# A GeGLU feed-forward layer: eight half-size products of the down projection become seven

## The chip, the core and the metric

The kernel runs on one core of a Trainium2 chip. The core has a matrix engine (TensorE, PE in the profile; its weight loads are listed apart as PEld), a vector engine (VectorE, DVE), an activation engine (ScalarE, ACT), GpSimd (POOL) and a queue engine (SyncE, SP) that issues most DMA transfers. Working data lies in SBUF, matrix results in PSUM, which has eight banks of 128 x 512 fp32 values. The metric is device time in microseconds of one execution; the time before is the median of five runs.

## The reference

The layer has 1024 tokens (32 x 32), width D = 1024 and inner width F = 3584. All inputs and the output are bf16.

```python
def _gelu(x):
    return jax.nn.gelu(x, approximate=True)

def reference(x, w_gate, w_up, w_down):
    return (_gelu(x @ w_gate) * (x @ w_up)) @ w_down
```

These are three products of the same size: x times w_gate, x times w_up, and the gated result g (1024 x 3584) times w_down (3584 x 1024).

## The kernel before

A tile is 128 rows or columns: F has 28 of them (FT), the tokens 8, D has 8. One matmul instruction multiplies a stationary 128 x 128 block (loaded by a weight load) by a moving block of up to 512 columns and adds the result to one PSUM bank.

**First stage.** x is brought in transposed (xT). The first quarter of D for the first 512 tokens is transposed on TensorE, the rest comes by transposing DMAs on SP. The weights w_gate and w_up are loaded in seven chunks of four F-tiles (1 MB each for wg and wu) into two rotating buffers. For each F-tile and each block of 512 tokens, 8 matmuls make a gate bank and 8 an up bank (`mm1`, line 117). `eltwise` (lines 125 to 138) turns the two banks into 512 columns of gT: ACT copies the gate (L127) and squares it (L129), DVE makes the argument of a sigmoid in two operations (L131, L133), ACT evaluates the sigmoid (L135), DVE multiplies with the up bank (L137) and with the sigmoid (L138). The eight PSUM banks hold four such pairs, so TensorE can be up to three pairs ahead of the elementwise work. The first chunk is written out by hand in another order ("head", lines 186 to 195): its four F-tiles share the pieces of x and the weights as they arrive.

w_down (wd, 7 MB) is loaded whole on SP, in seven loads of 1 MB, `load_wd`, during the first stage.

**Second stage.** `mm2_block` (line 209) takes one token tile and one half of D, accumulates 28 matmuls (line 212) in a bank, with gT stationary and wd moving, then DVE casts the bank to bf16 (L220) and ACT issues the store (L221). 8 token tiles by 2 halves give 16 blocks; the last one is cut in a block of 384 and one of 128 columns, which makes 17.

**Order.** TensorE's order around the head is as written (`manual_schedule` for that engine); the other engines are ordered by the framework's planner. Each engine and each DMA queue takes its instructions in order: one that waits holds up what is behind it.

Of the kernel before, what the change touches and what calls it, by code (L numbers as in the profile page):

```python
# [8 lines left out]
ACT = mybir.ActivationFunctionType  # L9
ALU = mybir.AluOpType  # L10

_C2 = 2.0 * 0.7978845608028654
_A = 0.044715
_C2A = _C2 * _A
# [3 lines left out]
def kernel(  # L18
# [8 lines left out]
    nc = tc.nc  # L27
    P = nc.NUM_PARTITIONS
    fp32 = mybir.dt.float32
    bf16 = mybir.dt.bfloat16  # L30

    xf = x.flatten_outer_dims()
    of = out.flatten_outer_dims()
    N, D = xf.shape
    F = w_gate.shape[1]
    assert D % P == 0 and F % P == 0 and N % P == 0
    DT = D // P
    FT = F // P
    NT = N // P
    MM_N = 512  # L40
    NB = min(N, MM_N)
    assert N % NB == 0
    NNB = N // NB
    DB = min(D, MM_N)
    assert D % DB == 0
    NDB = D // DB

    FC = 4
    assert FT % FC == 0 and DT % 4 == 0
    NCH = FT // FC  # L50
    KQ = DT // 4
    NWARM = 6
# [2 lines left out]
    wu_r = w_up.rearrange("(dt dp) f -> dp dt f", dp=P)  # L55
    wd_r = w_down.rearrange("(ft fp) d -> fp ft d", fp=P)

    xpool = ctx.enter_context(tc.tile_pool(name="xT", bufs=1))
    gpool = ctx.enter_context(tc.tile_pool(name="gT", bufs=1))
    wdpool = ctx.enter_context(tc.tile_pool(name="wd", bufs=1))  # L60
    wpool = ctx.enter_context(tc.tile_pool(name="w", bufs=2))
    ework = ctx.enter_context(tc.tile_pool(name="ework", bufs=3))
    opool = ctx.enter_context(tc.tile_pool(name="osb", bufs=3))
    cpool = ctx.enter_context(tc.tile_pool(name="const", bufs=1))
    pspool = ctx.enter_context(tc.tile_pool(name="psum", bufs=8, space=bass.MemoryType.PSUM))

    xT = xpool.tile([P, DT, N], bf16, name="xT")
    gT = gpool.tile([P, FT, N], bf16, name="gT")
    wd = wdpool.tile([P, FT, D], bf16, name="wd")

    ones_w = nc.const_aps.tensor(1.0, [P, P], bf16)
    ones_m = nc.const_aps.tensor(1.0, [P, NB], bf16)
    warm_ps = pspool.tile([P, NB], fp32, name="warm_ps", tag="acc")
# [3 lines left out]
    HALF = NB_P // 2  # L77
# [9 lines left out]
    def alloc_w_chunk(ci):  # L87
        w_tiles[ci] = (
            wpool.tile([P, DT, FC * P], bf16, name="wg", tag="wg"),
            wpool.tile([P, DT, FC * P], bf16, name="wu", tag="wu"),  # L90
        )

    def load_w(eng, ci, which, d0, d1):
        src = (wg_r, wu_r)[which]
        f0 = ci * FC * P
        eng.dma_start(out=w_tiles[ci][which][:, d0:d1, :], in_=src[:, d0:d1, f0 : f0 + FC * P])

    def load_w_chunk(ci):
        alloc_w_chunk(ci)
        for which in (0, 1):  # L100
            load_w(nc.sync, ci, which, 0, DT)

    def load_xT(t0, t1, d0, d1):
        nc.sync.dma_start_transpose(out=xT[:, d0:d1, t0:t1], in_=xf[t0:t1, d0 * P : d1 * P])

    def load_wd(ci):
        fsl = slice(ci * FC, (ci + 1) * FC)
        nc.sync.dma_start(out=wd[:, fsl, :], in_=wd_r[:, fsl, :])

    def weights_of(ft):  # L110
        fl = ft % FC
        fsl = slice(fl * P, (fl + 1) * P)
        return [t[:, :, fsl] for t in w_tiles[ft // FC]]

    def mm1(ps, wt, t0, tw, d0=0, d1=DT):
        for dt in range(d0, d1):
            nc.tensor.matmul(  # L117
                ps,
                lhsT=wt[:, dt, :],
                rhs=xT[:, dt, t0 : t0 + tw],  # L120
                start=(dt == 0),
                stop=(dt == DT - 1),
            )

    def eltwise(ft, t0, tw, gate_ps, up_ps):
        h = ework.tile([P, NB], bf16, name="h", tag="h")[:, :tw]
        nc.scalar.activation(h, gate_ps, ACT.Copy)  # L127
        sq = ework.tile([P, NB], bf16, name="sq", tag="sq")[:, :tw]
        nc.scalar.activation(sq, gate_ps, ACT.Square)  # L129
        w = ework.tile([P, NB], bf16, name="w", tag="w")[:, :tw]  # L130
        nc.vector.tensor_scalar(w, sq, _C2A, _C2, ALU.mult, ALU.add)  # L131
        z = ework.tile([P, NB], bf16, name="z", tag="z")[:, :tw]
        nc.vector.tensor_tensor(z, w, h, ALU.mult)  # L133
        s = ework.tile([P, NB], bf16, name="s", tag="s")[:, :tw]
        nc.scalar.activation(s, z, ACT.Sigmoid)  # L135
        hu = ework.tile([P, NB], bf16, name="hu", tag="hu")[:, :tw]
        nc.vector.tensor_tensor(hu, h, up_ps, ALU.mult)  # L137
        nc.vector.tensor_tensor(gT[:, ft, t0 : t0 + tw], hu, s, ALU.mult)  # L138

    def pair(tw):  # L140
        return (
            pspool.tile([P, NB], fp32, name="gate_ps", tag="acc")[:, :tw],
            pspool.tile([P, NB], fp32, name="up_ps", tag="acc")[:, :tw],
        )

    def mm1_and_eltwise(ft, t0, tw):
        ps = pair(tw)
        for p, wt in zip(ps, weights_of(ft)):
            mm1(p, wt, t0, tw)
        eltwise(ft, t0, tw, *ps)  # L150

    alloc_w_chunk(0)
    for dt in range(KQ):
        load_w((nc.sync, nc.scalar)[dt % 2], 0, 0, dt, dt + 1)
    load_w(nc.scalar, 0, 1, 0, KQ)
    for q in range(1, 4):
        d0, d1 = q * KQ, (q + 1) * KQ
        load_xT(0, NB, d0, d1)
        load_w(nc.sync, 0, 0, d0, d1)
        load_w(nc.sync, 0, 1, d0, d1)  # L160
    for nb in range(1, NNB):
        for q in range(2):
            load_xT(nb * NB, (nb + 1) * NB, 2 * q * KQ, 2 * (q + 1) * KQ)
    load_w_chunk(1)
    load_wd(0)

    with tc.manual_schedule(engines={mybir.EngineType.PE}):
        for _ in range(NWARM):
            nc.tensor.matmul(warm_ps, lhsT=ones_w, rhs=ones_m, start=True, stop=True)  # L169
        for dt in range(KQ):  # L170
            for half in range(2):
                hw = HALF * P
                tp = pspool.tile([P, hw], bf16, name="tp", tag="acc")
                for b in range(HALF):
                    nc.tensor.transpose(  # L175
                        tp[:, b * P : (b + 1) * P],
                        x_nat[:, half * HALF + b, dt * P : (dt + 1) * P],
                        ident,
                    )
                dst = xT[:, dt, half * hw : (half + 1) * hw]  # L180
                if half == 0:
                    nc.vector.tensor_copy(dst, tp)  # L182
                else:
                    nc.scalar.copy(dst, tp)  # L184
        nc.tensor.matmul(warm_ps[:, : NB // 2], lhsT=ones_w, rhs=ones_m[:, : NB // 2], start=True, stop=True)  # L185
        head = [pair(NB) for _ in range(FC)]
        for q in range(3):
            for which in (0, 1):
                for dt in range(q * KQ, (q + 1) * KQ):
                    for ft in range(FC):  # L190
                        mm1(head[ft][which], weights_of(ft)[which], 0, NB, dt, dt + 1)
        for ft in range(FC):
            for which in (0, 1):
                mm1(head[ft][which], weights_of(ft)[which], 0, NB, 3 * KQ, DT)
            eltwise(ft, 0, NB, *head[ft])

    for ft in range(FC):
        for nb in range(1, NNB):
            mm1_and_eltwise(ft, nb * NB, NB)

    for ci in range(1, NCH):
        if ci + 1 < NCH:
            load_w_chunk(ci + 1)
        load_wd(ci)
        for fl in range(FC):
            for nb in range(NNB):
                mm1_and_eltwise(ci * FC + fl, nb * NB, NB)

    def mm2_block(tsl, dsl):
        out_ps = pspool.tile([P, dsl.stop - dsl.start], fp32, name="out_ps", tag="acc")  # L210
        for ft in range(FT):
            nc.tensor.matmul(  # L212
                out_ps,
                lhsT=gT[:, ft, tsl],
                rhs=wd[:, ft, dsl],
                start=(ft == 0),
                stop=(ft == FT - 1),
            )
        o_sb = opool.tile([P, DB], bf16, name="o_sb", tag="o_sb")[:, : dsl.stop - dsl.start]
        nc.vector.tensor_copy(o_sb, out_ps)  # L220
        nc.scalar.dma_start(out=of[tsl, dsl], in_=o_sb)  # L221

    for tt in range(NT):
        tsl = slice(tt * P, (tt + 1) * P)
        for db in range(NDB):
            if tt == NT - 1 and db == NDB - 1 and DB > P:
                cut = (db + 1) * DB - P
                mm2_block(tsl, slice(db * DB, cut))
                mm2_block(tsl, slice(cut, (db + 1) * DB))
            else:  # L230
                mm2_block(tsl, slice(db * DB, (db + 1) * DB))


# [28 lines left out]
```

## Time and profile before

| | |
|---|---|
| median of five runs | 300.26 us (299.43 to 300.54) |
| the profiled execution | 300.19 us |
| its span, first to last instruction | 298.4 us |
| TensorE busy | 294.6 us (99%) |
| VectorE, ScalarE busy | 108.8 us (36%), 98.2 us (33%) |
| matmuls of the two up projections | 896, from 4.7 to 198.5 us |
| matmuls of the down projection | 476, from 198.5 to 295.2 us |
| DMA moved | 26.43 MB, mean 89 GB/s |

A group's line shows the program line, the engine and operation, output and inputs, the shape and the count, then the busy time in us and the mean duration in ns of one instruction, then the idle time of the engine just before them and what ended it. A matmul's duration includes its way through the array, which overlaps with that of the next; how often one starts is read from the chain in order of time. Line numbers are those of the kernel before.

### The profile page before, as it was taken

What the parts mean: (1) busy time and instruction counts of PE and PEld (TensorE: products, weight loads), DVE (VectorE), ACT (ScalarE), POOL (GpSimd) and SP (SyncE); (2) the same over time, 40 slices, a digit from 0 to 9 for tenths busy, and PEclk for the clock granted to TensorE, in tenths of its full rate; (3) what the DMA queues carried; (4) which work ended last, traced back from release to release, by engine and by line L of the source; (5) the groups of instructions that cost most, each with busy time, mean ns of one, the idle gap of its engine ahead of it and who ended that gap; (6) DMA issues with size and microseconds to landing.
All of it is one profiled execution on the core that took longest, in us unless ns stands there. A gap on an engine that the chain in (4) does not pass through costs nothing.

```text
span 298.4 us, 3493 instructions
## 1 busy us (share of the span) xinstructions
PE 294.6 (99%) x1387; PEld 134.7 (45%) x1387; DVE 108.8 (36%) x243; ACT 98.2 (33%) x172; POOL 0.7 (0%) x6
## 2 busy tenths in 40 slices
PE   8999999999999999999999999999999999999996
PEld 3444444444444444444444444444444444444444
DVE  0057654445554445554445555440010001100111
ACT  2087544554544554544554454540000000000000
POOL 0000000000000000000000000000000000000000
PEclk9999999999999999999999999999999999999999
DMA  7999996080026005300800000000001000000001
GB/s 162 313 282 379 387 366 227 0 281 2 0 74 207 2 0 170 111 2 2 279 4 0 0 0 2 0 0 18 20 18 35 18 20 18 34 21 18 18 18 37
DMA packets 28703, 26.43 MB, mean 89 GB/s; under 512 B 8208, under 2 KB 25104, under 8 KB 28688
## 3 DMA queue, kind: packets, MB, share of 16 engines
q1 hardware_dynamic: 25552, 23.60, 24.7%
q10 hardware_dynamic: 3136, 2.62, 2.9%
q8 instruction: 11, 0.18, 0.2%
q14 instruction: 4, 0.03, 0.0%
HBM read 22.28 MB, written 2.10 MB: 82 GB/s over the span
## 4 chain that ended last, share of the span: by engine, by line
PE 98%; DMA 1%; DVE 0%; issue 0%
PE gate_ps L117 32%; PE up_ps L117 32%; PE out_ps L212 32%; DMA x_nat<-in_x_dram 1%; PE tp L175 0%; DVE o_sb L220 0%; PE warm_ps L185 0%
## 5 line engine op out<-in xcount | busy, mean ns | idle before, releaser
L117 PE MATMUL gate_ps<-xT,wg 128*128 128x512 bf16 x448 | 106.6, 380 | 0.0
L117 PE MATMUL up_ps<-xT,wu 128*128 128x512 bf16 x448 | 106.3, 379 | 0.0
L212 PE MATMUL out_ps<-wd,gT 128*128 128x512 bf16 (+2 forms) x476 | 96.9, 366 | 0.0
L212 PEld LDWEIGHTS <-gT 128*128 128x128 bf16 x476 | 45.5, 98 | 51.6
L117 PEld LDWEIGHTS <-wg 128*128 128x128 bf16 x448 | 43.9, 98 | 52.9 <-issue 0.3
L117 PEld LDWEIGHTS <-wu 128*128 128x128 bf16 x448 | 43.8, 98 | 53.1 <-DMA wu<-in_w_up_dram 0.5
L127 ACT ACTIVATE h<-gate_ps 128x512 bf16<-128x512 f32 x56 | 33.4, 597 | 52.3 <-PE gate_ps L117 52.3
L135 ACT ACTIVATE s<-z 128x512 bf16<-128x512 bf16 x56 | 35.3, 630 | 46.1 <-DVE z L133 46.1
L131 DVE TENSOR_SCALAR w<-sq 128x512 bf16<-128x512 bf16 x56 | 16.5, 294 | 74.6 <-ACT sq L129 74.5
L137 DVE TENSOR_TENSOR hu<-h,up_ps 128x512 bf16<-128x512 bf16 x56 | 38.2, 681 | 12.0 <-ACT h L127 12.0
L220 DVE CAST o_sb<-out_ps 128x512 bf16<-128x512 f32 (+2 forms) x17 | 11.2, 660 | 84.4 <-PE out_ps L212 84.4
L129 ACT ACTIVATE sq<-gate_ps 128x512 bf16<-128x512 f32 x56 | 33.1, 592 | 0.0
L138 DVE TENSOR_TENSOR gT<-hu,s 128x512 bf16<-128x512 bf16 x56 | 23.8, 426 | 9.9 <-ACT s L135 9.9
L133 DVE TENSOR_TENSOR z<-w,h 128x512 bf16<-128x512 bf16 x56 | 23.8, 425 | 1.8
L169 PE MATMUL warm_ps<-const-bfloat16-1.0 128*128 128x512 bf16 x6 | 2.7, 624 | 0.8 <-PEq L246 0.8
L182 DVE COPY xT<-tp 128x256 bf16<-128x256 bf16 x2 | 0.6, 293 | 4.2 <-PE tp L175 4.2
L184 ACT ACT_TABLE_LOAD x1 | 1.3, 1283 | 2.3 <-issue 2.3
L169 PEld LDWEIGHTS <-const-bfloat16-1.0 128*128 128x128 bf16 x6 | 0.7, 132 | 1.9 <-issue 1.9
L135 ACT ACT_TABLE_LOAD x1 | 1.3, 1283 | 0.0
L175 PEld LDWEIGHTS <-x_nat 128*128 128x128 bf16 x8 | 0.7, 130 | 1.1 <-DMA x_nat<-in_x_dram 1.0
L175 PE MATMUL tp<-ident,x_nat 128*128 128x128 bf16 x8 | 1.1, 307 | 0.1
L184 ACT COPY xT<-tp 128x256 bf16<-128x256 bf16 x2 | 0.7, 372 | 0.8 <-PE tp L175 0.7
(8 smaller groups left out, 1.5 us busy)
## 6 DMA issues: line engine op xcount, KB each, us to landing
wd<-in_w_down_dram SPq DMA_DIRECT2D x7, 1024.0 KB, 14.0
wg<-in_w_gate_dram SPq DMA_DIRECT2D x6, 1024.0 KB, 5.3
wu<-in_w_up_dram SPq DMA_DIRECT2D x6, 1024.0 KB, 7.3
out_dram<-o_sb ACTq DMA_DIRECT2D x15, 128.0 KB, 1.7
wg<-in_w_gate_dram SPq DMA_DIRECT2D x3, 256.0 KB, 3.8
wu<-in_w_up_dram SPq DMA_DIRECT2D x3, 256.0 KB, 4.2
wu<-in_w_up_dram ACTq DMA_DIRECT2D x1, 256.0 KB, 5.0
x_nat<-in_x_dram ACTq DMA_DIRECT2D x1, 128.0 KB, 3.1
```

The lines of the kernel that those rows point to most:

```text
L117: nc.tensor.matmul(ps, lhsT=wt[:, dt, :], rhs=xT[:, dt, t0 : t0 + tw], start=(dt == 0), stop=(dt == DT - 1),)
L127: nc.scalar.activation(h, gate_ps, ACT.Copy)
L129: nc.scalar.activation(sq, gate_ps, ACT.Square)
L131: nc.vector.tensor_scalar(w, sq, _C2A, _C2, ALU.mult, ALU.add)
L133: nc.vector.tensor_tensor(z, w, h, ALU.mult)
L135: nc.scalar.activation(s, z, ACT.Sigmoid)
L137: nc.vector.tensor_tensor(hu, h, up_ps, ALU.mult)
L138: nc.vector.tensor_tensor(gT[:, ft, t0 : t0 + tw], hu, s, ALU.mult)
L169: nc.tensor.matmul(warm_ps, lhsT=ones_w, rhs=ones_m, start=True, stop=True)
L184: nc.scalar.copy(dst, tp)
L212: nc.tensor.matmul(out_ps, lhsT=gT[:, ft, tsl], rhs=wd[:, ft, dsl], start=(ft == 0), stop=(ft == FT - 1),)
L220: nc.vector.tensor_copy(o_sb, out_ps)
```

## The change

Three things change.

**The down projection.** g and w_down are cut in halves: A11 and A12 are the tokens 0 to 511 with the F-tiles 14 to 27 and 0 to 13, A21 and A22 the tokens 512 to 1023 likewise; B11, B12 are the rows of the F-tiles 14 to 27 of w_down with the columns 0 to 511 and 512 to 1023, B21, B22 those of the F-tiles 0 to 13. Eight products of such halves would give the output. The new kernel makes seven (Winograd's form of Strassen's method): A12 B21, A11 B11, S1 T1, S2 T2, S3 T3, A22 T4 and S4 B22, in this order. The sums are

- S1 = A21 + A22, S2 = S1 - A11, S3 = A11 - A21, S4 = A12 - S2
- T1 = B12 - B11, T2 = B22 - T1, T3 = B22 - B12, T4 = B21 - T2

A half-size product is 4 token tiles (m) by 14 F-tiles (k) of 128 x 128 x 512 matmuls. It occupies four PSUM banks; there are two sets of four, banka and bankb, and several products accumulate on top of an earlier one in the same set. Copies of a bank's intermediate state are taken by ACT into SBUF (`snap`), and DVE adds them to the final banks when it writes the output (`store`).

The sums are made on DVE from bf16 into tiles of type float32r (4 bytes). The five products with a sum in them run with both operands in float32r; for two of these ACT copies A22 and B22 into float32r tiles. S2 and T2, T4 and S4 are made in place. S1 and T1 are made during the first stage, the other sums during the second.

**The loads of w_down.** It is no longer kept whole in SBUF. A ring of four buffers of 512 KB (`wdring`) receives batches of four F-tiles by 512 columns (the last of a half has two F-tiles). Each batch is loaded on SP when it is wanted, several of them more than once: 8 loads in the first stage, 28 in the second. A load waits until the reader of the buffer four loads earlier is done.

**GELU and order.** `eltwise` is one GELU activation on ACT and one product on DVE. All engines, not TensorE alone, keep the order in which the program is written.

The core of the diff, with the first stage's unchanged lines left out:

```diff
     def eltwise(ft, t0, tw, gate_ps, up_ps):
         h = ework.tile([P, NB], bf16, name="h", tag="h")[:, :tw]
-        nc.scalar.activation(h, gate_ps, ACT.Copy)
-        sq = ework.tile([P, NB], bf16, name="sq", tag="sq")[:, :tw]
-        nc.scalar.activation(sq, gate_ps, ACT.Square)
-        w = ework.tile([P, NB], bf16, name="w", tag="w")[:, :tw]
-        nc.vector.tensor_scalar(w, sq, _C2A, _C2, ALU.mult, ALU.add)
-        z = ework.tile([P, NB], bf16, name="z", tag="z")[:, :tw]
-        nc.vector.tensor_tensor(z, w, h, ALU.mult)
-        s = ework.tile([P, NB], bf16, name="s", tag="s")[:, :tw]
-        nc.scalar.activation(s, z, ACT.Sigmoid)
-        hu = ework.tile([P, NB], bf16, name="hu", tag="hu")[:, :tw]
-        nc.vector.tensor_tensor(hu, h, up_ps, ALU.mult)
-        nc.vector.tensor_tensor(gT[:, ft, t0 : t0 + tw], hu, s, ALU.mult)
+        nc.scalar.activation(h, gate_ps, ACT.Gelu_apprx_tanh)
+        nc.vector.tensor_tensor(g_of(ft)[:, t0 : t0 + tw], h, up_ps, ALU.mult)
...
+    HF = FT // 2
+    HT = N // 2
+    MT = HT // P
+    KB = 4
+    batches = [(k, min(k + KB, HF)) for k in range(0, HF, KB)]
+    hi, lo = HF, 0
+    A11, A12 = [[g[:, :, :HT] for g in gs] for gs in (g_hi, g_lo)]
+    A21, A22 = [[g[:, :, HT:] for g in gs] for gs in (g_hi, g_lo)]
+
+    def load_b(f_off, col, b):
+        k0, k1 = b
+        t = wdring.tile([P, KB, DB], bf16, name="wdb", tag="wdb")
+        nc.sync.dma_start(
+            out=t[:, : k1 - k0, :],
+            in_=wd_r[:, f_off + k0 : f_off + k1, col * DB : (col + 1) * DB],
+        )
+        return t[:, : k1 - k0, :]
...
             for fl in range(FC):
                 for nb in range(NNB):
                     mm1_and_eltwise(ci * FC + fl, nb * NB, NB)
+                for i, b in enumerate(batches):
+                    sl = slice(*b)
+                    if ci * FC + fl == FC * (3 + i):
+                        b11, b12 = load_b(hi, 0, b), load_b(hi, 1, b)
+                        tt(tch[:, sl, :], b12, b11, ALU.subtract)
+                    if ci * FC + fl == HF - 1 + b[1]:
+                        tt(sch[:, sl, :], A21[b[0] // KB], A22[b[0] // KB], ALU.add)
+
+        first.close()
...
+        def product(banks, lhs, rhs, start, head=0, tail=0):
+            def mm(k, m):
+                nc.tensor.matmul(
+                    banks[m],
+                    lhsT=lhs(k)[:, m * P : (m + 1) * P],
+                    rhs=rhs(k),
+                    start=(start and k == 0),
+                    stop=(k == HF - 1),
+                    skip_group_check=True,
+                )
+            for k0, k1 in ((0, head), (head, HF - tail), (HF - tail, HF)):
+                if k0 == head:
+                    for k in range(k0, k1):
+                        for m in range(MT):
+                            mm(k, m)
+                else:
+                    for m in range(MT):
+                        for k in range(k0, k1):
+                            mm(k, m)
...
+        def snap(banks, name):
+            out = []
+            for ps in banks:
+                t = snaps.tile([P, DB], fp32, name=name, tag=name)
+                nc.scalar.copy(t, ps)
+                out.append(t)
+            return out
+
+        def store(m, tok, col, in0, in1):
+            o = opool.tile([P, DB], bf16, name="o_sb", tag="o_sb")
+            if in1 is None:
+                nc.scalar.copy(o, in0)
+            else:
+                tt(o, in0, in1, ALU.add)
+            t0 = tok * HT + m * P
+            nc.scalar.dma_start(out=of[t0 : t0 + P, col * DB : (col + 1) * DB], in_=o)
...
+        b21 = [load_b(lo, 0, b) for b in batches]
+        bankb = banks_of("bankb")
+        product(bankb, by_batch(A12), by_batch(b21), True)
+        sb = snap(bankb, "snb")
+        for b in batches:
+            sl = slice(*b)
+            tt(s3[:, sl, :], A11[b[0] // KB], A21[b[0] // KB], ALU.subtract)
+
+        def t3_of(b):
+            b22, b12 = load_b(lo, 1, b), load_b(hi, 1, b)
+            tt(t3[:, b[0] : b[1], :], b22, b12, ALU.subtract)
+
+        b11 = []
+        for b in batches:
+            if b[0] < 2 * KB:
+                t3_of(b)
+            b11.append(load_b(hi, 0, b))
+        banka = banks_of("banka")
+        product(banka, by_batch(A11), by_batch(b11), True)
+        for m in range(MT):
+            store(m, 0, 0, sb[m], banka[m])
+        product(bankb, by_k(sch), by_k(tch), True)
+        s5 = snap(bankb, "snb")
+        for b in batches:
+            sl = slice(*b)
+            b22 = load_b(lo, 1, b)
+            tt(tch[:, sl, :], b22, tch[:, sl, :], ALU.subtract)
+            tt(sch[:, sl, :], sch[:, sl, :], A11[b[0] // KB], ALU.subtract)
+        product(banka, by_k(sch), by_k(tch), False, tail=4)
+        s2 = snap(banka, "sna")
+        for b in batches[2:]:
+            t3_of(b)
+        product(banka, by_k(s3), by_k(t3), False, head=4, tail=4)
+        for b in batches:
+            sl = slice(*b)
+            tt(tch[:, sl, :], load_b(lo, 0, b), tch[:, sl, :], ALU.subtract)
+        a22r = g_tiles("hi_r", f32r, HT)
+        for b in batches:
+            sl = slice(*b)
+            nc.scalar.copy(a22r[b[0] // KB], A22[b[0] // KB])
+        for m in range(MT):
+            store(m, 1, 1, s5[m], banka[m])
+        product(banka, by_batch(a22r), by_k(tch), False, tail=HF)
+        b22r = g_tiles("lo_r", f32r, DB)
+        for b in batches:
+            sl = slice(*b)
+            tt(sch[:, sl, :], A12[b[0] // KB], sch[:, sl, :], ALU.subtract)
+            nc.scalar.copy(b22r[b[0] // KB], load_b(lo, 1, b))
+        for m in range(MT):
+            store(m, 1, 0, banka[m], None)
+        product(bankb, by_k(sch), by_batch(b22r), False, tail=HF)
+        for m in range(MT):
+            store(m, 0, 1, s2[m], bankb[m])
```

`tt` is VectorE's two-operand operation; `sch` holds S1, then S2, then S4, `tch` holds T1, then T2, then T4; `s3`, `t3` hold S3 and T3 and lie in the memory that xT and the first stage's weights had. The float32r copies a22r and b22r take the memory of the halves of g that are no longer read. Only the ordering of the sum's operands and places matters for what follows; the first stage's matmuls are unchanged.

## The prediction

> **What bounds the kernel now.** I read the page's busy table first, then the chain that ended last, then the chain in order of time for where the stages begin, then the groups kept apart by form.
>
> ```profile
> PE 294.6 (99%) x1387; PEld 134.7 (45%) x1387; DVE 108.8 (36%) x243; ACT 98.2 (33%) x172; POOL 0.7 (0%) x6
> ...
> PEclk9999999999999999999999999999999999999999
> ...
> PE gate_ps L117 32%; PE up_ps L117 32%; PE out_ps L212 32%; DMA x_nat<-in_x_dram 1%; PE tp L175 0%; DVE o_sb L220 0%; PE warm_ps L185 0%
> ```
>
> TensorE is never idle, its granted clock is full throughout, and the chain is matmuls in three equal parts. Only fewer or cheaper matmuls shorten this kernel.
>
> ```profile
> 195.21 1.73 PE gate_ps L117 x8
> 196.94 1.73 PE up_ps L117 x8
> 198.67 96.78 PE out_ps L212 x476
> ```
>
> Eight 512-column matmuls take 1.727 us (195.21 to 196.94): 0.216 us each. The 380 ns of the groups is one matmul's whole length; they overlap. The down projection begins at 198.5 (its first matmul in the timeline) and holds 96.75 us, 448 full-width equivalents.
>
> ```profile
> L212 PEld LDWEIGHTS <-gT 128*128 128x128 bf16 x476 | 45.5, 98 | 51.6
> ...
> L137 DVE TENSOR_TENSOR hu<-h,up_ps 128x512 bf16<-128x512 bf16 x56 | 38.2, 681 | 12.0 <-ACT h L127 12.0
> ...
> L127 ACT ACTIVATE h<-gate_ps 128x512 bf16<-128x512 f32 x56 | 33.4, 597 | 52.3 <-PE gate_ps L117 52.3
> ...
> L220 DVE CAST o_sb<-out_ps 128x512 bf16<-128x512 f32 x15 | 10.4, 692 | 79.6 <-PE out_ps L212 79.6
> ...
> L184 ACT COPY xT<-tp 128x256 bf16<-128x256 bf16 x2 | 0.7, 372 | 0.8 <-PE tp L175 0.7
> ...
> L220 DVE CAST o_sb<-out_ps 128x128 bf16<-128x128 f32 x1 | 0.3, 291 | 1.0 <-PE out_ps L212 1.0
> ```
>
> The DMA issues of the window from 84 to 96, and from the timeline the last DVE instruction of the kernel:
>
> ```profile
> wg<-in_w_gate_dram SPq DMA_DIRECT2D x1, 1024.0 KB, 5.2
> wu<-in_w_up_dram SPq DMA_DIRECT2D x1, 1024.0 KB, 7.2
> ```
>
> ```profile
> 295.47 0.29 DVE L220 CAST o_sb<-out_ps 128x128 bf16<-128x128 f32 x1 [1.00 <-PE out_ps L212]
> ```
>
> These are my prices. Weight loads run beside matmuls (98 ns inside 216). DVE at one element a cycle: (692 - 291)/384 = 1.044 ns an element plus 157 ns, so 2048 elements (four k-tiles of 512) cost 2.30 us, 1024 cost 1.23, and one sum over 14 k-tiles 3 x 2.30 + 1.23 = 8.1 us. No row has a sum with a 4-byte result; the two-operand bf16 product z, 425 ns against 681, suggests 1.2 us as the low end, and I take 2.30 because each row with 4-byte data (hu, the CAST) runs at that rate. ACT: (597 - 372)/256 = 0.88 ns an element plus 147 ns, so 0.60 us for 512 and 1.95 for 2048. DMA: the two 1 MB loads issued 1.7 us apart at 86.5 and 88.2 move some 345 GB/s once running, so 1 MB is 3.0 us of data and 2.2 fixed, and 512 KB about 3.7 us alone and 1.5 more for each queued ahead.
>
> **The change, part by part.**
>
> Matmuls: seven products of 4 x 14 = 56 make 392, at 0.216 us 84.6 us against 96.75: minus 12.1 us. Two products stay bf16 (112 matmuls), five are float32r (280). No float32r matmul is in the trace. Bounds: below, the bf16 0.216 us, as no row suggests that wider operands go faster; above, whole extra passes, 280 x 0.216 = 60.5 us each (three more: 181). Between them lies the weight load: 98 ns, hidden now; fully exposed it adds 280 x 0.098 = 27.4 us. I take 0.216 with hidden loads, because the nearest row is the same 128x128 by 512 shape, and its load could double and still fit inside the matmul. This is the largest uncertainty.
>
> The Trainium skill speaks against this step: "TensorE: Matmul & The Clock Gate", Weight-path perf modes, says that fast weight load is off for FP32 operands, and its LDWEIGHTS section gives columns/1.2 ns, an estimated 107 ns for 128, which still fits under 216 and leaves the sum as it is. "FP8 and Floating Point Precision", TensorE Precision Notes, separates reduced-precision FP32 (truncated on reading) from true FP32 in four passes; by the second the estimate is 181 us more. No run here shows either yet.
>
> GELU in one activation: ACT goes from three operations per tile to one (GELU is in no row; a copy takes 597 ns and the sigmoid 630, so 0.6, and twice that would hide as well), DVE from four to one (0.68), in the first stage. Neither was late there (TensorE's idle is 0.0), so the gain is nothing. The activation table load (1.28 us) lies in front of the first GELU, while ACT waits 11 us for it. In their place DVE gets T1 (8.1 us) and S1 (8.1): 38 + 16 = 54 us of DVE in some 194, less than today's 102. The T1 piece after F-tile 12 waits on DVE for two w_down loads queued behind a 2 MB weight chunk, about 9.5 us after that tile begins; the eltwise behind it slips to 12 us, while its PSUM pair is needed again only at 20.7. Cost nothing; with a second 10 us delay it would show. Removing the seven 1 MB w_down loads from SP's queue, and ordering all engines by hand, gain nothing: SP's order in the trace is the program's already.
>
> Product 1 (A12 B21) starts at 198.5 with everything loaded, until 210.6.
>
> Product 2 is where I expect a stall. Its first B11 batch goes into ring slot 2, free when product 1 has finished k-tiles 8 to 11, at 198.5 + 48 x 0.216 = 208.9 plus 0.15. Landing 3.7 us later, at 212.75, it makes TensorE wait 2.2 us. The second B11 batch is behind it on SP: b12 of the second T3 batch, then b11, both wait until DVE ends the first T3 piece. DVE: last GELU product 199.5, last S1 piece 200.8, S3 (8.1) 209.1, T3 piece 211.6. From then three 512 KB loads follow one another; b11 lands near 217.4, while k-tiles 0 to 3 end at 216.25: 1.2 us more. Batches three and four land at 220.1 and 221.5, before their use at 220.9 and 224.4. Together 3.4 us. Below: 0 (all hidden); above: 6, with 1 MB durations for 512 KB.
>
> Here a rule would add to it. The trace shows a slower TensorE at the start, six warm-up matmuls in 2.72 us, 0.43 us apart, twice 0.216. The same clock-gate page (The two states you'll see) puts that half rate behind some 3.4 us without work; my longest gap, 2.2 us, would not reach it, but a gap beyond it would cost an estimated 1.7 us more (half of 3.4 us at half rate).
>
> Products 3 to 5: S1 and T1 are ready. T2 and S2 are made in place behind product 3: eight DVE operations, 2 x 8.1 = 16.2 us, starting when product 3 has read its first four k-tiles. With product 3 from 226.1 they run from 229.8 to 246.1. Product 4 starts at 238.2, asks for k-tile 8 at 245.1 (ready 243.6) and for 12 at 247.3: margins of 1.5 and 1.1 us. Cost nothing; this is the thinnest cover. S3 and T3 lie where x and the first stage's weights were, so they wait for its last matmul (198.5), before DVE comes to them anyway. The remaining T3 pieces end at 249.6, product 5 asks for them near 254. ACT's snapshots (0.60) follow bank by bank, since products 4 and 5 finish and start with whole banks at 0.86 us each: nothing.
>
> Products 6 and 7: T4, S4 (8.1 us of DVE each) and the two float32r copies on ACT (6.9 us each) fit in the 12.1 us of the product before. Product 6 writes bank 3 again 0.65 us after product 5 ends, while its store needs about 0.95 on DVE: 0.3 us of stall. The stores' DMA triggers on ACT sit ahead of the copies of B22, which wait for S4 on DVE anyway.
>
> Tail: product() with tail=HF and head=0 has its last range at k0 = head = 0, so it takes the k-outer branch: four banks finish together. Four DVE adds of 0.69 us follow, the last ending 2.4 us after TensorE against 0.5 now, and a 128 KB store lands 0.2 us later than a 32 KB one (1.7 to 1.5): plus 2.1 us.
>
> The 28 loads of w_down in this stage are 12.5 MB, some 36 us at 345 GB/s in 88: past product 2 they follow the ring with time to spare. DVE here: one S1 piece 1.2, six sums of 8.1, twelve combining operations of some 0.69 at most: 58 us in 88. Not the bound in total.
>
> The sum: the profiled execution took 300.19 us (span 298.4 and 1.8 around it). 300.19 - 12.1 + 3.4 + 0.3 + 2.1 = 293.9. The runs' median is 300.26, 0.07 more, so **294.0 us**, 2.1% faster.
>
> **The rivals.**
>
> Exposed weight loads (the other side). The gain before float32r is 6.3 us, over 280 matmuls 22 ns each. If a float32r matmul is 22 ns slower than 0.216 us there is no gain; if its load can't run beside the matmul before, 98 ns each give 294.0 + 27.4 = 321 us. For: the trace shows only bf16 loads hidden, and the operands are twice as wide. Against: 45% busy weight loads leave room for double.
>
> Float32r in several passes: two give 354 us, four 475. For: nothing in the trace excludes it. Against: nothing speaks for it either.
>
> A slightly slower float32r matmul, 5 to 20 ns more: 295.4 to 299.6.
>
> DVE and the loads become late: eight in-place operations at 2.75 us in place of 2.30 take 3.6 more, 1.1 of it covered: 296.5. Product 2's loads at their upper end add 2.6 us (296.6), a clock drop there 1.7 more. Together about 301. For: the margins. Against: the CAST rows are a one-element-a-cycle price already.
>
> The stores do go bank by bank and loads are hidden: 294.0 - 1.9 - 1.9 = 290.2, the low end; I count it inside the forecast.
>
> **How the numbers follow.** Forecast (float32r like bf16) 0.66, 290.5 to 297; slightly slower matmuls 0.07; DVE or loads late 0.09, 296 to 303; exposed loads 0.10; several passes 0.08. The last two, 0.18, stay outside: range 290.5 to 303. A measurement of this kernel can tell about 0.2%. Faster: 0.66 + 0.07 + 0.04 of the late case = 0.77; within 0.2%: 0.02; slower: 0.03 + 0.18 = 0.21.
>
> **What would show it.** Start-to-start of the float32r matmuls (0.216, or 0.24 and up); weight loads' time and whether they are separate instructions; two gaps on TensorE before product 2 of about 2.2 and 1.2 us, released by a w_down DMA; none between products 3 and 5; DVE sums of 2.30 us; 2.4 us of DVE after the last matmul; clock full throughout. A float32r matmul over 22 ns slower than bf16, or DVE sums over 3 us, make the prediction wrong.

## The result, and the profile after

The changed kernel takes 298.5 us (median of 26 runs, 297.2 to 301.6) against 300.1 (46 runs, 299.4 to 300.7): a ratio of 0.9957, 95% interval 0.9943 to 0.9972. It is 0.4% faster; 2.1% was forecast. The profiled execution took 297.77 us, with a span of 295.8. One thing is needed to read the median: its executions form two groups, 14 between 297.2 and 298.6 us with a mean granted clock of 0.996 or more, and 12 between 299.4 and 301.6 with 0.989 to 0.994.

First the page of the profiled execution: busy time, the granted clock, the chain's shares.

```profile
PE 286.0 (97%) x1303; PEld 152.6 (52%) x1303; DVE 109.5 (37%) x102; ACT 58.6 (20%) x84; POOL 0.7 (0%) x6
...
PEclk9999999999999999999999999999999999999999
...
PE 93%; DMA 3%; DVE 1%; DVEq 0%; issue 0%; SPq 0%
PE gate_ps L137 33%; PE up_ps L137 33%; PE banka L247 16%; PE bankb L247 11%; DMA wdb<-in_w_down_dram 3%; PE warm_ps L191 1%; DVE t L298 1%; DVE o_sb L281 1%; PE tp L197 0%; DVEq L366 0%; SPq L168 0%; PE warm_ps L207 0%; DVEq L281 0%; DVEq L298 0%
```

The chain is still TensorE for 93%, but w_down loads have come into it. The same chain in order of time (start, length, what) shows where:

```profile
196.71 1.73 PE up_ps L137 x8
198.44 6.92 PE bankb L247 x32
205.36 0.02 issue
205.37 3.31 DMA wdb<-in_w_down_dram
...
208.77 2.30 DVE t L298
...
211.09 0.38 SPq L168
...
211.52 6.96 DMA wdb<-in_w_down_dram
...
218.53 8.79 PE banka L247 x40
227.32 12.72 PE bankb L247 x56
240.04 25.40 PE banka L247 x112
...
266.27 12.35 PE banka L247 x53
278.62 12.71 PE bankb L247 x56
...
292.62 0.60 DVE o_sb L281
```

Product 1 starts at once. Then the chain leaves TensorE: a load of B12 (L168), the first T3 piece on DVE (L298), SP's next issue, and a load that lands 7 us later, for which product 2 waits until 218.53. From there matmuls follow with one short break, 0.3 us in product 6 (its third slot ends at 265.94, the next matmul starts at 266.27); but 56 of float32r take 12.72 us, where 56 of bf16 take 12.09.

TensorE's own timeline gives the gaps, in brackets the idle time before a stretch and what ended it:

```profile
198.27 12.25 PE L247 MATMUL bankb<-wdb,lo 128*128 128x512 bf16 x56
212.19 3.63 PE L247 MATMUL banka<-wdb,hi 128*128 128x512 bf16 x16 [1.66 <-DMA wdb<-in_w_down_dram]
218.53 8.79 PE L247 MATMUL banka<-wdb,hi 128*128 128x512 bf16 x40 [2.71 <-DMA wdb<-in_w_down_dram]
```

Counted from the end of the last matmul's slot (its start plus 0.216 us) the gaps are 1.8 and 2.9 us, 4.7 together. And the groups by form:

```profile
L247 PE MATMUL banka<-tch,sch 128*128 128x512 f32 x56 | 12.9, 389 | 0.0
...
L247 PE MATMUL bankb<-wdb,lo 128*128 128x512 bf16 x56 | 12.2, 379 | 0.0
...
L247 PEld LDWEIGHTS banka<-tch,sch 128*128 128x128 f32 x56 | 10.5, 188 | 2.2
...
L314 DVE TENSOR_TENSOR tch<-wdb,tch 128x2048 fp32r<-128x2048 bf16 x3 | 6.9, 2288 | 1.7 <-PE bankb L247 1.7
```

A float32r weight load takes 188 ns in place of 98, a separate instruction beside the matmul as in bf16. DVE's pieces take 2.29 us.

### The profile page after: what moved, and what is told of

Read it like the earlier page. It is cut to its first block, busy times and chain, and to the rows that moved or that the text cites. A ratio compares the mean times of both kernels' runs of the same rounds, so it can differ in the third digit from the quotient of the medians.

```text
span 295.8 us, 3126 instructions
## 1 busy us (share of the span) xinstructions
PE 286.0 (97%) x1303; PEld 152.6 (52%) x1303; DVE 109.5 (37%) x102; ACT 58.6 (20%) x84; POOL 0.7 (0%) x6
## 4 chain that ended last, share of the span: by engine, by line
PE 93%; DMA 3%; DVE 1%; DVEq 0%; issue 0%; SPq 0%
PE gate_ps L137 33%; PE up_ps L137 33%; PE banka L247 16%; PE bankb L247 11%; DMA wdb<-in_w_down_dram 3%; PE warm_ps L191 1%; DVE t L298 1%; DVE o_sb L281 1%; PE tp L197 0%; DVEq L366 0%; SPq L168 0%; PE warm_ps L207 0%; DVEq L281 0%; DVEq L298 0%
## 5 line engine op out<-in xcount | busy, mean ns | idle before, releaser
L148 DVE TENSOR_TENSOR lo<-h,up_ps 128x512 bf16<-128x512 bf16 x28 | 19.2, 687 | 74.7 <-PE up_ps L137 62.3
L148 DVE TENSOR_TENSOR hi<-h,up_ps 128x512 bf16<-128x512 bf16 x28 | 19.2, 687 | 59.9 <-PE up_ps L137 59.9
L247 PE MATMUL banka<-wdb,hi 128*128 128x512 bf16 x56 | 12.4, 379 | 4.4 <-DMA wdb<-in_w_down_dram 4.4
L247 PE MATMUL banka<-tch,hi_r 128*128 128x512 f32 x56 | 13.2, 392 | 0.2 <-DVE o_sb L281 0.2
L247 PE MATMUL bankb<-tch,sch 128*128 128x512 f32 x56 | 13.1, 393 | 0.0
L247 PE MATMUL banka<-tch,sch 128*128 128x512 f32 x56 | 12.9, 389 | 0.0
L247 PE MATMUL banka<-t,s 128*128 128x512 f32 x56 | 12.9, 389 | 0.0
L247 PE MATMUL bankb<-lo_r,sch 128*128 128x512 f32 x56 | 12.9, 389 | 0.0
L247 PE MATMUL bankb<-wdb,lo 128*128 128x512 bf16 x56 | 12.2, 379 | 0.0
L247 PEld LDWEIGHTS bankb<-tch,sch 128*128 128x128 f32 x56 | 10.5, 188 | 2.3
```

Of the source, the lines that this page charges most:

```text
L148: nc.vector.tensor_tensor(g_of(ft)[:, t0 : t0 + tw], h, up_ps, ALU.mult)
L247: nc.tensor.matmul(banks[m], lhsT=lhs(k)[:, m * P : (m + 1) * P], rhs=rhs(k), start=(start and k == 0), stop=(k == HF - 1), skip_group_che ...
```

## The experiments

The theory after the result: the order of the loads in the ring makes both gaps; gaps that get a little longer let the clock fall, which makes the upper group; float32r costs 11 ns a matmul.

**The loads of product 2 in another order.** B11 is loaded first, one T3 piece is made before S2 and T2 and three after.

```diff
-        b11 = []
-        for b in batches:
-            if b[0] < 2 * KB:
-                t3_of(b)
-            b11.append(load_b(hi, 0, b))
+        b11 = [load_b(hi, 0, b) for b in batches]
+        t3_of(batches[0])
...
-        for b in batches[2:]:
+        for b in batches[1:]:
             t3_of(b)
```

> Only the order of the w_down loads around product 2 changes: the four B11 batches are loaded first, then the loads of the first T3 piece; the other three T3 pieces are made after S2 and T2. The changed kernel's trace has two gaps on TensorE before and in product 2, 1.8 and 2.9 us. Theory: both are the ring's order alone, so they go, 4.7 us off the 297.5 us that the changed kernel takes when its granted clock is 0.999: 292.8 us. And the gaps are what lets the clock fall (0.993 in about half of its executions, some 2.3 us longer), so here it stays at 0.999 or more in every run and the runs agree within 0.5 us. Rival: the float32r matmuls themselves bring the clock down; then half of the runs still lie 2 us above the others with a clock of 0.993.

Measured: 293.18 us, five runs between 293.02 and 293.75; ratio 0.9772, 0.9756 to 0.9789. Its chain in order of time:

```profile
198.18 12.09 PE bankb L247 x56
210.26 12.09 PE banka L247 x56
222.35 12.72 PE bankb L247 x56
235.07 25.40 PE banka L247 x112
```

Products 1 and 2 now touch. The gaps were the ring's order, and with them the upper group is gone: none of these five runs shows it, nor any of the 13 runs of the three forms below that build on this order (bf16 sums, bank by bank with the new order, all of it together). One part was missed: the runs lie 0.7 us apart, not within 0.5, and in three of the five the mean clock is 0.996, though one of the three is the fastest of the five. In the profile of the changed kernel the clock is 0.95 in the last 4.5 us, when no matmul is left; such a drop costs nothing, but that it is the one of these three runs was not traced.

**How the clock comes in.** Two more executions of the changed kernel were profiled.

> The changed kernel once more, unchanged, for a profile of an execution with the lower clock. Theory: if this execution takes about 299.9 us, its granted clock is 0.993 and falls to half within a few us behind the second gap (2.9 us) in product 2, nowhere else, and the matmuls there are 0.43 us apart; if it takes about 297.5 us, there is no such stretch. Rival: the low stretch lies at the start of the kernel or in the float32r products.

> The same kernel as the run before it, a second look, with the same expectation: 299.9 us with half the clock behind the second gap, or 297.5 us without.

Measured: 298.21 us with a clock of 1.000, and 300.71 us with 0.993. The second one's timeline of TensorE, and stretches of 2 us with the busy time of each engine, then the granted clock, the DMA share and GB/s:

```profile
212.58 3.63 PE L247 MATMUL banka<-wdb,hi 128*128 128x512 bf16 x16 [1.72 <-DMA wdb<-in_w_down_dram]
...
219.95 6.28 PE L247 MATMUL banka<-wdb,hi 128*128 128x512 bf16 x21 [3.74 <-DMA wdb<-in_w_down_dram]
```

```profile
216.00:218.00 2.00, 0.21 (x1) 0.00 (x0) 0.98 (x1) 0.00 (x0) 0.00 (x0) 1.00 0.90 280
218.00:220.00 2.00, 0.05 (x1) 0.05 (x1) 1.31 (x1) 0.00 (x0) 0.00 (x0) 0.83 0.61 206
220.00:222.00 2.00, 2.00 (x5) 0.65 (x5) 0.00 (x0) 0.00 (x0) 0.00 (x0) 0.50 0.68 195
222.00:224.00 2.00, 2.00 (x9) 0.88 (x8) 0.00 (x0) 0.00 (x0) 0.00 (x0) 0.81 0.59 208
224.00:226.00 2.00, 1.95 (x10) 0.89 (x10) 0.00 (x0) 0.00 (x0) 0.00 (x0) 1.00 0.00 0
```

In this execution the second gap, counted from the end of the last slot as above, is 3.9 us (the 3.74 in the bracket counts from the end of the last matmul's whole length), not 2.9, since the load before it landed 7.95 us after its issue and not 6.96. Near its end the clock falls to half, and it is full again at about 222.8 (0.81 over the stretch from 222 to 224 is 0.76 us at half). The 17 matmuls behind the gap take 5.20 us; in the first of the two, whose gap is 3.0 us, they take 3.83. So this execution of the upper group pays 1.0 us for a later load and 1.4 us for the clock. That the others of the group do the same is inferred from their lower mean clock and similar times. Why this load lands a microsecond later in some executions was not settled.

**Longer gaps on purpose.** A ring of three buffers.

```diff
-    wdring = ctx.enter_context(tc.tile_pool(name="wdring", bufs=4))
+    wdring = ctx.enter_context(tc.tile_pool(name="wdring", bufs=3))
```

> The changed kernel with a ring of three buffers for w_down in place of four, so that loads are later and TensorE's gaps longer. Theory: gaps above 3.4 us in product 2, the clock falls in every execution (0.993 or less, seen as a slice of the granted clock below full), and each fall costs about 2 us beside the gaps: 305 to 312 us. Rival: the clock has nothing to do with the gaps and lies at 0.993 in about half of the executions.

Measured: 306.99 us (304.2 to 308.5), clocks 0.978 three times and 0.993 once. The page's clock, and the chain:

```profile
PEclk9999999999999999999999999999569999999999
```

```profile
210.09 4.76 DMA wdb<-in_w_down_dram
214.85 0.05 issue
214.90 5.88 PE banka L247 x16
...
220.80 3.69 DMA wdb<-in_w_down_dram
224.49 0.04 issue
224.53 6.37 PE banka L247 x17
```

Sixteen matmuls that take 3.63 us at full clock (the changed kernel's timeline) take 5.88 behind the first gap, of 5.0 us, and 17, which take 3.83, take 6.37 behind the second, of 3.9 us: 2.2 and 2.5 us more. A fall does not have one price, then; the one above cost 1.4. Each run shows a lower clock, so the gaps bring it down, and float32r, which runs later at a full clock, does not.

**Float32r against bf16.** With the new order of loads, the type of the sums and of the two copies changed.

```diff
-    f32r = mybir.dt.float32r
+    f32r = mybir.dt.bfloat16
```

> As the kernel with the B11 batches loaded first, but the sums and the two copies are bf16 instead of float32r (the sums are rounded to bf16, which is the part of the computation that changes). Theory: a float32r matmul starts every 0.227 us and a bf16 one every 0.216, so 280 x 0.011 = 3.1 us go: 289.7 us, weight loads back at 98 ns. Rival: the longer spacing comes from DVE and ACT working in SBUF beside the matmuls, not from the type; then the spacing stays near 0.227 and the time at 292.8.

Measured: 289.78 us, 3.4 less than with float32r; ratio 0.9652, 0.9635 to 0.9669. The chain from product 2 to 5, then two groups:

```profile
210.41 12.09 PE banka L247 x56
222.49 12.09 PE bankb L247 x56
234.58 24.19 PE banka L247 x112
```

```profile
L247 PE MATMUL bankb<-tch,sch 128*128 128x512 bf16 x56 | 12.2, 379 | 0.0
...
L311 DVE TENSOR_TENSOR tch<-wdb,tch 128x2048 bf16<-128x2048 bf16 x3 | 3.7, 1225 | 3.5 <-PE bankb L247 3.5
```

The spacing is back at 0.216 us in every product. DVE's pieces halve too (1.22 us), but they were hidden. With that, DVE works less beside the matmuls than before, so this run alone does not put the rival out. The profile of the changed kernel does, in two stretches, the first with product 1 (bf16), the second with product 7 (float32r); the columns are length, then the busy time of PE, PEld, DVE, ACT and POOL:

```profile
198.20:210.40 12.20, 12.20 (x58) 5.39 (x55) 11.28 (x7) 0.49 (x2) 0.00 (x0) 1.00 0.27 94
278.50:291.30 12.80, 12.80 (x57) 10.29 (x55) 0.57 (x1) 1.82 (x4) 0.00 (x0) 1.00 0.12 41
```

Beside product 1 DVE is busy for 11.28 us, most of it writing float32r sums, and matmuls start every 0.216 us; beside product 7 it is busy for 0.57 us, and they start every 0.227 (12.71/56). So it is the type.

**What the 11 ns depend on.** Each float32r matmul in two of 256 columns, with the new order of loads.

```diff
-                nc.tensor.matmul(
-                    banks[m],
+                cuts = (0, DB) if lhs(k).dtype == bf16 else (0, DB // 2, DB)
+                for c0, c1 in zip(cuts, cuts[1:]):
+                    nc.tensor.matmul(
+                        banks[m][:, c0:c1],
                         lhsT=lhs(k)[:, m * P : (m + 1) * P],
-                    rhs=rhs(k),
+                        rhs=rhs(k)[:, c0:c1],
```

> As the kernel with the B11 batches loaded first, but each float32r matmul is cut into two of 256 columns (560 in place of 280, each with its own weight load). It asks what the 11 ns are. If a fixed cost per matmul: spacing 0.107 + 0.011 = 0.118, plus 280 x 0.011 = 3.1 us, 296 us. If per column (5%): spacing 0.1135, no change, 292.8. If the 188 ns weight load limits as soon as the matmul is shorter than it: spacing about 0.19, 280 x (0.38 - 0.227) = 43 us more, 336 us.

The two halves of a bank are started separately here, which changes what the bank accumulates; the instructions are the same in number and kind otherwise. Measured, in a single execution: 297.34 us. Chain and a group:

```profile
223.31 13.43 PE bankb L249 x112
236.74 26.89 PE banka L249 x224
```

```profile
L249 PEld LDWEIGHTS banka<-tch,sch 128*128 128x128 f32 x112 | 13.5, 192 | 0.0
```

Spacing 26.89/224 = 0.120 us. Had the cost been per column, it would be 0.1135; as a fixed cost, 0.118. The two spacings say the same: from 512 columns to 256 the spacing falls by 0.107 us, so another 0.107 belongs to the 256 columns that are left, and 0.013 does not depend on columns; if a column costs bf16 as much, its 0.216 leaves 0.002. And matmuls start every 0.120 us although a weight load lasts 0.192, so these overlap one another: the length of one load is not the limit. A fixed 11 to 13 ns a matmul fits best. It is not shown beyond doubt: the weight loads follow each other without a pause here (PEld is busy for 27.00 of the 27.00 us from 236 to 263), so the rate of the loads could also set the 0.120. What in TensorE the 11 ns are, no run separates.

**Products 6 and 7 bank by bank**, alone, and with the new order of loads.

```diff
-                if k0 == head:
+                if k0 == head and tail < HF:
```

> The changed kernel with products 6 and 7 bank by bank and nothing else. Theory: minus 0.6 us before product 6 and minus 1.0 at the end, 295.9 us where the clock is 0.999; the gaps of product 2 stay, so about half of the runs lie some 2.3 us higher with a clock of 0.993. Rival: the end is set by the stores, then minus 0.6 only.

> As the kernel with the B11 batches loaded first, and products 6 and 7 go bank by bank. Theory: product 6 no longer waits 0.6 us for the store of bank 3, and after the last matmul one DVE addition is left in place of four, about 1.0 us less: 291.2 us. Rival: the end is set by the last stores' DMAs and not by DVE, then the tail gives nothing and the time is 292.2.

Measured: alone 297.52 us (eight runs, 296.6 to 300.5), ratio 0.9930, 0.9896 to 0.9965, the gaps and a spread of clocks still there. The 295.9 us expected of the faster executions were missed: the six faster runs lie between 296.6 and 298.0. In the profiled one TensorE comes to product 1 at 198.95, 0.7 us later than in the changed kernel's profile, and the second gap is longer, 3.2 us:

```profile
212.90 3.63 PE L247 MATMUL banka<-wdb,hi 128*128 128x512 bf16 x16 [1.71 <-DMA wdb<-in_w_down_dram]
219.58 8.79 PE L247 MATMUL banka<-wdb,hi 128*128 128x512 bf16 x39 [3.05 <-DMA wdb<-in_w_down_dram]
```

The granted clock is 1.00 over this gap, so the step lies between 3.2 and 3.9 us. From product 3 to the end of the span the profile is 1.6 us shorter than the changed kernel's, as the theory says; the later start and the longer gap hide a part of it. Three of the six faster runs have a mean clock of 0.994, so the mean clock alone does not tell the two groups apart here.

With the new order the time is 291.8 us (291.35 to 292.17), ratio 0.9720, 0.9703 to 0.9737: 1.4 us below the new order alone. The end of this one:

```profile
236.11 38.08 PE banka L247 x168
274.19 12.71 PE bankb L247 x56
286.89 0.04 DVEq L281
286.93 0.05 issue
286.98 0.69 DVE o_sb L281
```

The three products on banka run without a break (38.08/168 = 0.227 us), and one addition of 0.69 us is left behind the last matmul. The median lies nearer to the rival's 292.2 than to the theory's 291.2. But in the rival the tail gives nothing, and the traces show that it does: from the end of the last matmul to the end of the span it is 3.3 us (286.89 to 290.2), with the new order alone 4.8 us (286.32 to 291.1).

**GELU alone**, in the kernel before.

```diff
-        nc.scalar.activation(h, gate_ps, ACT.Copy)
...
-        nc.vector.tensor_tensor(gT[:, ft, t0 : t0 + tw], hu, s, ALU.mult)
+        nc.scalar.activation(h, gate_ps, ACT.Gelu_apprx_tanh)
+        nc.vector.tensor_tensor(gT[:, ft, t0 : t0 + tw], h, up_ps, ALU.mult)
```

> The kernel before with nothing changed but GELU as one activation and one product on DVE. Theory: ACT and DVE were not late, so 300.1 us, within 0.3 of before. Rival: the shorter chain from a gate bank to its release, or fewer PSUM and SBUF accesses, gives TensorE something: 298 to 299.

Measured: 300.39 us, ratio 1.0001, 0.9991 to 1.0012. Nothing, as forecast.

**All of it together**: new order, bank by bank, bf16 sums.

> B11 batches loaded first, products 6 and 7 bank by bank, and the sums and copies in bf16 (sums rounded to bf16). Theory: the three savings lie on TensorE one behind the other and add up: the 289.8 us of the bf16 form minus the 1.4 us that bank by bank gave (293.2 to 291.8) is 288.4 us, 3.9% below before. Rival: with bf16 sums DVE's part is shorter and the tail partly hidden already, then about 289.

Measured: 288.76 us (287.9 to 289.0), ratio 0.9616, 0.9594 to 0.9638, within its runs' spread of either figure. This form rounds the sums to bf16; the one that keeps float32r is the 291.8 us above, and it too beats both kernels.

## Why the prediction was wrong

Summed from the profiled execution, against 300.19 us:

| step | forecast | measured | from |
|---|---|---|---|
| 56 matmuls fewer | -12.1 | -12.1 | 56 x 0.216 |
| float32r | 0 | +3.2 | products 3 to 7, 227.17 to 291.15, less 280 x 0.216 and the 0.3 below |
| product 2's loads | +3.4 | +4.7 | gaps 1.8 and 2.9 |
| product 6 | +0.3 | +0.3 | third slot's end 265.94 to 266.27 |
| tail | +2.1 | +1.5 | end of the last slot to the span's end, 4.65 less 3.15 |
| start of the stage, time around the span | 0 | 0.0 | -0.2 and +0.2 |
| sum | -6.3 | -2.4 | 297.77 |

The mechanism was right, the likeliest case was not. Two steps failed.

**"I take 0.216 with hidden loads."** The loads are hidden, and float32r takes a single pass. But a float32r matmul starts 11 ns later than a bf16 one would, 280 times: 3.2 us by the profile, 3.4 by the medians with and without bf16 sums. The nearest row, of another type, could not show it. The text had named this as a rival (5 to 20 ns more, at 0.07). The 22 ns from which there is no gain was the right yardstick: half of it was used up here. The Trainium skill, "TensorE: Matmul & The Clock Gate", LDWEIGHTS, gave an estimated 107 ns for the load; it measured 188. What the same page says under Weight-path perf modes, that fast weight load is off for FP32, fits the direction: 188 ns here against 98 with bf16. Of the two cases in "FP8 and Floating Point Precision", TensorE Precision Notes, the four passes are ruled out by the spacing of 0.227 us.

**"1.2 us more" for the second gap, and the clock above it.** The first gap was sized well (2.2, measured 1.8). For the second I had three loads of 512 KB landing 1.5 us apart, the last at 217.4, and product 2's first 16 matmuls ending at 216.25; they ended at 215.64 and the load landed at 218.5. Both errors add to the gap. A part of the first was in the sum: three loads that follow one another from 211.6, where the prediction has the first T3 piece end, land by its own 3.7 and twice 1.5 us at 218.3, not at 217.4. The clock was named, with a threshold that "my longest gap, 2.2 us, would not reach". With gaps up to 3.2 us it does not fall; with 3.9 it does. So the second gap, 1.7 us longer than forecast, came near the step, and a load that lands one microsecond later, which I had not priced, takes an execution over it. About half of the executions lie in the upper group, some 2.3 us higher, which is why the median is 298.5 and not 297.6. "TensorE: Matmul & The Clock Gate" of the Trainium skill (The two states you'll see) puts the fall behind some 3.4 us without work, which agrees with 3.2 and 3.9 on either side. The cost, which I estimated from it at 1.7 us, measured 1.4, and 2.2 and 2.5 with the ring of three.

Right were: nothing from GELU (1.0001); S1 and T1 in the first stage at no cost; T2 and S2 on time (no gap between products 3 and 5, pieces of 2.29 us against 2.30); the snapshots; the order in which product() takes the last products, and that it costs something. The tail was sized too high, and by luck this took 0.6 us off the other two errors: the first of the four additions starts 0.6 us before TensorE is done (290.73 against 291.33), and they follow each other at 0.6 us, not 0.69.

That late loads and slow matmuls were one rival each, at 0.09 and 0.07, was the other mistake: they came together, in a kernel with 280 instructions of a kind that the trace had never shown and a ring of four buffers under the eight loads of product 2 and the first T3 pieces. The measured median lies inside the range (290.5 to 303), but outside the 290.5 to 297 of the likeliest case: 1.6 us were gained, where 6.3 were forecast. Neither of the two signs that the prediction named for being wrong came, since float32r cost 11 ns a matmul and not 22, and DVE's sums took 2.29 us and not 3. Its low end does not follow from its sum: without the 3.4 us for the loads and the 2.1 for the tail, 294.0 becomes 288.5, not 290.2.

## What to carry to other kernels

An instruction in a type that the trace does not show has an unknown fixed cost even if its rate is the same: divide the expected gain by the number of such instructions and ask whether that many nanoseconds can be excluded. Where a ring's loads are issued in program order, put first what the matrix engine needs next, not what a helper needs later: this alone was worth 5.3 us of 298.5. And price a gap on TensorE with a step in it: in this kernel, somewhere between 3.2 and 3.9 us, a gap began to cost 1.4 to 2.5 us more, and a kernel near the step shows a median that hides two groups.

## What the runs showed of the hardware

- Float32r matmuls of 128x128 by 512 start every 0.227 us, by 256 every 0.120; bf16 by 512 every 0.216. Their weight loads take 188 to 192 ns (bf16 98) and overlap one another.
- A gap of 3.9 us on TensorE brought the granted clock to 0.50 until about 2.9 us after the matmuls resumed; gaps of 2.9, 3.0 and 3.2 us did not.
- A sum of two 2048-element operands on DVE takes 2.29 us with a 4-byte result and 1.22 with everything in bf16.
- Of three 512 KB loads issued one behind the other, the last landed 6.96 to 7.95 us after its issue; the median over the 27 loads of this size is 4.0.
